# Sliding-window attention and a highway layer on one core: constants set up early, separate PSUM buffers for H and Z, x of two duos transposed by DMA

## The chip, the core and the metric

The kernel runs on one core of a Trainium2 chip. A core has five engines that run their own instruction streams and wait for each other by semaphores: TensorE (PE, matmuls, with weight loads as PEld), VectorE (DVE), ScalarE (ACT), GpSimd (POOL) and SyncE (SP, which here only issues DMAs). Matmul results go to PSUM, everything else lies in SBUF. The metric is the device time of one execution in microseconds, as a median of several runs. The span of a profile is a little shorter than that time (188.6 us against 190.34 us for the profiled run).

## What is computed

Eight heads of attention over 576 positions, causal, with a window of 128 and a bias that falls with the distance, and behind it a highway layer on the joined heads:

```python
# q, k, v: (8, 8, 576, 64)
scores = scale * np.matmul(q, k.transpose(0, 1, 3, 2))
rel = pos[:, None] - pos[None, :]
bias = slopes[:, None, None] * (-np.abs(rel))[None]
mask = (rel >= 0) & (rel < 128)
scores = np.where(mask, scores + bias[None], -1e9)
attn = softmax(scores)
x = (attn @ v) as (4608, 512)           # tokens x joined heads

H = np.maximum(x @ w_h, 0.0)
T = 1.0 / (1.0 + np.exp(-(x @ w_t + b_t)))
out = T * H + (1.0 - T) * x             # = T * (H - x) + x
```

## The kernel before

Two batch rows make a *duo*; there are four duos, 0 to 3. Each duo is worked on in *stages*: A (query blocks 0 and 1) and B (query blocks 2, 3 and the half block 4); duo 0 has four smaller ones, a to d. All stages together give 36 *blocks* of 128 tokens for the highway layer, 9 for each duo.

For every stage and head, TensorE computes scores (L299), ScalarE the exponential (L314), VectorE multiplies two heads with a mask (L324), TensorE multiplies with v (PV, L347), and VectorE divides by the sum (the norm, L363 and L364), which gives x of the stage. Ahead of that, q and k are transposed on TensorE (L234, L248) and copied out of PSUM (L260, L267, L273). Then each block goes through the highway layer:

```python
def f_x(m, kind, b):                    # x transposed on TensorE (L378)
    pt = ps_tile(BF16)
    for c in range(NCK):                # NCK = 4
        nc.tensor.transpose(out=pt[:, 0, c * P : (c + 1) * P],
                            in_=X[m, kind][:, b, c * P : (c + 1) * P], identity=ident[:])

def f_xe(m, kind, b):                   # and copied to SBUF by ScalarE (L386)
    xt = fx.tile([P, NCK, P], BF16, name="xt")
    nc.scalar.copy(out=xt[:], in_=TR[m, kind, b][:, 0, 0:512]...)

def f_h(m, kind, b):                    # H: first half of a PSUM tile (L394)
    az = ps_tile()
    for c in range(NCK):
        nc.tensor.matmul(out=az[:, 0, :], lhsT=XT[m, kind, b][:, c, :], rhs=wH[:, c, :], ...)

def f_u(m, kind, b):                    # u = max(H, 0) - x (L400)
    nc.vector.scalar_tensor_tensor(out=uu[:], in0=AZ[m, kind, b][:, 0, :], scalar=0.0,
                                   in1=X[m, kind][:, b, :], op0=ALU.max, op1=ALU.subtract)

def f_z(m, kind, b):                    # Z: second half of the same tile (L408, bias L410)
    az = AZ[m, kind, b]
    for c in range(NCK):
        nc.tensor.matmul(out=az[:, 1, :], lhsT=XT[m, kind, b][:, c, :], rhs=wT[:, c, :], ...)
    nc.tensor.matmul(out=az[:, 1, :], lhsT=ones1[:], rhs=bT[:], start=False, stop=True)

def f_th(m, kind, b):                   # tanh(Z / 2) (L415)
    nc.scalar.activation(out=tt[:], in_=AZ[m, kind, b][:, 1, :], func=ACTF.Tanh, scale=0.5)

def f_t(m, kind, b):                    # T = tt / 2 + 1/2 (L419)
    nc.gpsimd.tensor_scalar(out=tt[:], in0=tt[:], scalar1=0.5, scalar2=0.5, ...)

def f_g(m, kind, b):                    # the gate: u * T (L424)
    nc.vector.tensor_tensor(out=uu[:], in0=uu[:], in1=TT.pop((m, kind, b))[:], op=ALU.mult)

def f_out(m, kind, b):                  # the sum: u * T + x, in float32 (L429)
    nc.gpsimd.tensor_tensor(out=ot[:], in0=UU.pop((m, kind, b))[:], in1=X[m, kind][:, b, :], ...)

def f_st(m, kind, b):                   # four stores (L443), or two for a half block (L438)
    ...
```

PSUM is given out as four slots of two banks each, for scores, PV, transposes and the highway layer alike:

```python
psp = ctx.enter_context(tc.tile_pool(name="ps", bufs=BUFS["ps"], space=PSUM))   # 4
def ps_tile(dt=F32):
    return psp.tile([P, 2, 512 if dt == F32 else 1024], dt, name="ps")
```

All of these pieces are nodes with an engine, an estimated duration, a priority and what they depend on. A list scheduler in the kernel's Python puts them in an order when the kernel is built; the constants `SHIFT` and `LOOKS` tune its priorities. Each engine then runs its instructions in exactly that order. Loads of q, k and v convert float32 to bf16 and are issued by GpSimd (L101, L106, L113), stores by SyncE.

```python
node("ident", "POOL", 500, -120, c_ident)
node("tri", "POOL", 2200, -84, c_tri)              # triangles for the masks, set to 1 on GpSimd
...
node(("kpad", 0), "DVE", 450, 5 * T, lambda: c_kpad(0))
node(("vpad", 0), "DVE", 930, 6 * T, lambda: c_vpad(0))
...
node(("x", kb), "ACT", 590, t - 0.9 * dt, lambda kb=kb: f_xe(*kb), [("xp", kb)], take="xt", ...)
node(("h", kb), "PE", 870, t, lambda kb=kb: f_h(*kb), [("x", kb), ("wc",)], take="ps", ...)
node(("z", kb), "PE", 1100, t + 0.5 * dt, lambda kb=kb: f_z(*kb), [("h", kb), ("w", 1), ("w", 2)], ...)
```

Of the kernel before, what the change touches and what calls it, by code (L numbers as in the profile page):

```python
# [10 lines left out]
P = 128  # L11
# [3 lines left out]
def kernel(  # L15
# [36 lines left out]
    DMA_X = ()  # L52
# [4 lines left out]
        "ps": 4, "pA": 6, "pB": 3, "pf": 9, "x": 3, "xt": 5, "uu": 3, "tt": 3, "ot": 3,  # L57
# [3 lines left out]
        n: ctx.enter_context(tc.tile_pool(name="p" + n, bufs=BUFS["p" + n])) for n in "ABf"  # L61
# [59 lines left out]
    kk_f = cp.tile([P, 1], F32, name="kk_f")  # L121
    BIAS = cp.tile([P, H], F32, name="bias")
    tri = cp.tile([P, 3, P], BF16, name="tri")
    MK = cp.tile([P, H, 512], BF16, name="mk")
    cvec = cp.tile([P, H], F32, name="cvec")
# [13 lines left out]
    def c_tri():  # L139
        nc.gpsimd.memset(tri[:], 1.0)  # L140

        for cols, pat, base, cm in (
            (tri[:, 0, :], [[1, 4], [4, 32]], 0, -1),
            (tri[:, 1, :], [[-1, 4], [-4, 32]], -1, 1),
            (tri[:, 2, 0:D], [[-1, D]], -1, 1),
            (tri[:, 2, D:P], [[1, D]], 0, -1),
        ):
            nc.gpsimd.affine_select(
                out=cols, in_=cols, compare_op=ALU.is_ge, fill=0.0,
                base=base, pattern=pat, channel_multiplier=cm,  # L150
            )
# [63 lines left out]
    TR, SC, PT, AV, X, XT, AZ, UU, TT, OT = ({} for _ in range(10))  # L215
# [65 lines left out]
    def scores(m, kind, h):  # L281
# [7 lines left out]
        segs, n = STAGES[kind], 0  # L289
        while n < len(segs):  # L290
            j, qb, off = segs[n]
            two = n + 1 < len(segs) and segs[n + 1][0] == j and segs[n + 1][1] < 4
            for r in range(2):
                rows = slice(r * D, (r + 1) * D)
                if qb == 4:
                    rhs, w_ = QT[i][rows, h, 512:S], D
                else:
                    rhs, w_ = qm[rows, qb : qb + 1 + two], P * (1 + two)
                nc.tensor.matmul(  # L299
                    out=sc[:, r, o + off : o + off + w_],  # L300
                    lhsT=KT[i][rows, h, j * P : (j + 1) * P],
                    rhs=rhs, start=True, stop=True,
                )
            n += 1 + two

    def soft(m, kind, h):
        W = width(kind)
        if h % 2 == 0:
            pt = ptp[kind if W == 512 else "f"].tile([P, 2, 2, W], BF16, name="pt")
            PT[m, kind, h // 2] = pt  # L310
            for j, qb, off in STAGES[kind]:
                COL[m, h // 2, j, qb] = (pt, off)
        o = 0 if W == 512 else (h % 2) * W
        nc.scalar.activation(  # L314
            out=PT[m, kind, h // 2][:, h % 2], in_=SC[m, kind, h][:, :, o : o + W],
# [4 lines left out]
    def mask(m, kind, g):  # L320
        rep, lo, W = {"A": (4, 0, 256), "B": (2, 0, 512), "d": (2, 256, 256)}.get(kind, (2, 0, 256))
        o = PT[m, kind, g][:].rearrange("p h r (j w) -> p h (r j) w", w=W)
# [46 lines left out]
    def f_xd(m, kind, b):  # L369
        xt = fx.tile([P, NCK, P], BF16, name="xt")  # L370
        XT[m, kind, b] = xt
        nc.sync.dma_start_transpose(out=xt[:], in_=X[m, kind][:, b, :])

    def f_x(m, kind, b):
        pt = ps_tile(BF16)
        TR[m, kind, b] = pt
        for c in range(NCK):
            nc.tensor.transpose(  # L378
                out=pt[:, 0, c * P : (c + 1) * P],
                in_=X[m, kind][:, b, c * P : (c + 1) * P], identity=ident[:],  # L380
            )

    def f_xe(m, kind, b):
        xt = fx.tile([P, NCK, P], BF16, name="xt")
        XT[m, kind, b] = xt
        nc.scalar.copy(  # L386
            out=xt[:], in_=TR[m, kind, b][:, 0, 0:512].rearrange("p (c n) -> p c n", c=NCK)
        )

    def f_h(m, kind, b):  # L390
        az = ps_tile()
        AZ[m, kind, b] = az
        for c in range(NCK):
            nc.tensor.matmul(out=az[:, 0, :], lhsT=XT[m, kind, b][:, c, :], rhs=wH[:, c, :],  # L394
                             start=c == 0, stop=c == NCK - 1)

    def f_u(m, kind, b):
        uu = ft.tile([P, DM], BF16, name="uu")
        UU[m, kind, b] = uu
        nc.vector.scalar_tensor_tensor(  # L400
            out=uu[:], in0=AZ[m, kind, b][:, 0, :], scalar=0.0, in1=X[m, kind][:, b, :],
# [3 lines left out]
    def f_z(m, kind, b):  # L405
        az = AZ[m, kind, b]
        for c in range(NCK):
            nc.tensor.matmul(out=az[:, 1, :], lhsT=XT[m, kind, b][:, c, :], rhs=wT[:, c, :],  # L408
                             start=c == 0, stop=False)
        nc.tensor.matmul(out=az[:, 1, :], lhsT=ones1[:], rhs=bT[:], start=False, stop=True)  # L410

    def f_th(m, kind, b):
        tt = ft.tile([P, DM], F16, name="tt")
        TT[m, kind, b] = tt
        nc.scalar.activation(out=tt[:], in_=AZ[m, kind, b][:, 1, :], func=ACTF.Tanh, scale=0.5)  # L415

    def f_t(m, kind, b):
        tt = TT[m, kind, b]
        nc.gpsimd.tensor_scalar(out=tt[:], in0=tt[:], scalar1=0.5, scalar2=0.5,  # L419
                                op0=ALU.mult, op1=ALU.add)  # L420

    def f_g(m, kind, b):
        uu = UU[m, kind, b]
        nc.vector.tensor_tensor(out=uu[:], in0=uu[:], in1=TT.pop((m, kind, b))[:], op=ALU.mult)  # L424

    def f_out(m, kind, b):
        ot = op.tile([P, DM], F32, name="ot")
        OT[m, kind, b] = ot
        nc.gpsimd.tensor_tensor(out=ot[:], in0=UU.pop((m, kind, b))[:], in1=X[m, kind][:, b, :],  # L429
                                op=ALU.add)  # L430

    def f_st(m, kind, b):
        ot = OT.pop((m, kind, b))
        r, qb = blocks(kind)[b]
        if qb == 4:
            for r in range(2):
                row = (2 * m + r) * S + 512
                nc.sync.dma_start(out=out[row : row + D, :], in_=ot[r * D : (r + 1) * D, :])  # L438
        else:
            row = (2 * m + r) * S + qb * P  # L440
            dst = out[row : row + P, :].rearrange("(p t) n -> t p n", t=4)
            for t in range(4):
                nc.sync.dma_start(out=dst[t], in_=ot[32 * t : 32 * t + 32, :])  # L443
# [16 lines left out]
    node("tri", "POOL", 2200, -84, c_tri)  # L460
    node("cbias", "ACT", 1500, -88, c_bias, ["ident"])
    node("cvec", "DVE", 1300, -90, c_vec)
    node(("ones", 0), "DVE", 300, -85, lambda: c_ones(0))
    node("mask0", "DVE", 1900, -50, lambda: c_mask(0), ["tri", "cvec"])
    node("mask1", "DVE", 1500, 5 * T, lambda: c_mask(1), ["tri", "cvec"])
    node(("kpad", 0), "DVE", 450, 5 * T, lambda: c_kpad(0))
    node(("vpad", 0), "DVE", 930, 6 * T, lambda: c_vpad(0))
    node(("ones", 1), "DVE", 300, 7 * T, lambda: c_ones(1))
    node(("vpad", 1), "DVE", 930, 8 * T, lambda: c_vpad(1))
    node(("kpad", 1), "DVE", 450, 9 * T, lambda: c_kpad(1))  # L470
# [6 lines left out]
    HALF = {"A": (330, 1118, 1340, 420, 950), "B": (370, 1118, 1340, 960, 1080),  # L477
# [8 lines left out]
    last_pv = {}  # L486
    for m in range(ND):
# [56 lines left out]
        for kind in ORDER[m]:  # L544
# [3 lines left out]
            for g in range(H // 2):  # L548
# [12 lines left out]
                pring = "p" + (kind if W == 512 else "f")  # L561
                for hl in range(2):
                    h = 2 * g + hl
                    tk = ("s", m, kind, h if W == 512 else 2 * g)
                    if tk[3] == h:
                        hs = (h,) if W == 512 else (h, h + 1)
                        node(tk, "PE", C[0] * len(hs), tg + (hl - 1.3) * U,
                             lambda m=m, kind=kind, hs=hs: [scores(m, kind, h) for h in hs],
                             need, take="ps")
                    node(("exp", m, kind, h), "ACT", C[1], tg + (hl - 1.2) * U,  # L570
                         lambda m=m, kind=kind, h=h: soft(m, kind, h), [tk, "cbias"] + [("exp", m, kind, 2 * g)] * hl,
                         take=None if hl else pring, uses=[tk])
                node(("msk", key), "DVE", C[2], tg + U, lambda key=key: mask(*key),
# [143 lines left out]
```

The softmax here doesn't subtract the row's maximum and nothing guards it: scores larger than these inputs give would overflow.

## Time and profile before

| | value |
|---|---|
| time, median of 3 runs | 190.37 us (189.91 to 194.2) |
| span of the profile | 188.6 us |
| mean granted clock of TensorE | 0.988 |
| transposes of x on TensorE (L378) | 144, 14.2 us busy, mean 224 ns |
| their copies on ScalarE (L386) | 36, 20.5 us busy, mean 590 ns |
| the sum on GpSimd (L429) | 36, 46.7 us busy, mean 1297 ns |
| tanh waiting for u | 38.9 us in 34 waits |
| u waiting for the last matmul of Z | 26.3 us in 29 waits |

In the lines of the profile a piece is given by engine, line of the kernel, operation and tiles, as `uu<-ps,x` for u. The slices cut the span into 40 equal parts, and a digit is the busy share of a part in tenths. In the timeline the first two numbers are start and length in us, and what stands in brackets is how long the engine was idle before, and whose result ended that. Matmuls are pipelined, so a busy PE isn't always PE at its peak. In a list of busy time by stretches, the columns are the stretch, its length, the busy time of PE, PEld, DVE, ACT and POOL with the number of instructions, the granted clock, the share of the DMA engines, and GB/s.

### The profile page before, as it was taken

What the parts mean: (1) busy time and instruction counts of PE and PEld (TensorE: products, weight loads), DVE (VectorE), ACT (ScalarE), POOL (GpSimd) and SP (SyncE); (2) the same over time, 40 slices, a digit from 0 to 9 for tenths busy, and PEclk for the clock granted to TensorE, in tenths of its full rate; (3) what the DMA queues carried; (4) which work ended last, traced back from release to release, by engine and by line L of the source; (5) the groups of instructions that cost most, each with busy time, mean ns of one, the idle gap of its engine ahead of it and who ended that gap; (6) DMA issues with size and microseconds to landing.
All of it is one profiled execution on the core that took longest, in us unless ns stands there. A gap on an engine that the chain in (4) does not pass through costs nothing.

```text
span 188.6 us, 5196 instructions
## 1 busy us (share of the span) xinstructions
PE 152.3 (81%) x2108; PEld 96.1 (51%) x2132; DVE 136.9 (73%) x238; ACT 124.8 (66%) x178; POOL 122.0 (65%) x138
## 2 busy tenths in 40 slices
PE   0287769897899888899978889998988899979900
PEld 0265534554657445565654556665645565644400
DVE  5288876788859777899866678789676679764660
ACT  2557745866877777778797677886777767343310
POOL 7996424965989738977895256724264756564880
PEclk9999999999999999999999999999999999999995
DMA  4999999999999999999999912043030222433453
GB/s 164 219 183 190 162 128 133 196 190 148 185 178 225 223 197 175 139 200 225 229 172 188 103 41 76 20 99 98 20 87 26 59 70 56 103 81 86 111 128 94
DMA packets 70167, 25.50 MB, mean 135 GB/s; under 512 B 48128, under 2 KB 65024, under 8 KB 70144
## 3 DMA queue, kind: packets, MB, share of 16 engines
q0 software_dynamic: 62832, 14.68, 100.0%
q1 hardware_dynamic: 7312, 10.49, 21.1%
q8 instruction: 16, 0.26, 0.6%
q14 instruction: 7, 0.06, 0.1%
HBM read 30.41 MB, written 9.44 MB: 211 GB/s over the span
## 4 chain that ended last, share of the span: by engine, by line
PE 30%; DMA 19%; DVE 12%; ACT 12%; issue 11%; POOL 11%; SPq 1%; POOLq 1%; ACTq 0%; DVEq 0%
PE ps L394 11%; PE ps L408 10%; DMA kl<-in_k_dram 9%; DMA va<-in_v_dram 8%; DVE uu L400 7%; ACT pt L314 4%; ACT xt L386 4%; POOL ot L429 4%; DMA out_dram<-ot 3%; PE ps L410 3%; PE ps L248 2%; PE ps L347 2%; DVE pt L324 2%; ACT tt L415 2%; POOL ql L101 2%
## 5 line engine op out<-in xcount | busy, mean ns | idle before, releaser
L314 ACT ACTIVATE pt<-ps,bias 128x1024 bf16<-128x1024 f32 (+1 forms) x80 | 71.9, 951 | 6.2 <-PE ps L299 6.2
L429 POOL TENSOR_TENSOR ot<-uu,x 128x512 f32<-128x512 bf16 x36 | 46.7, 1297 | 22.9 <-DVE uu L424 22.8
L415 ACT ACTIVATE tt<-ps 128x512 f16<-128x512 f32 x36 | 21.5, 597 | 39.0 <-DVE uu L400 38.9
L400 DVE SCALAR_TENSOR_TENSOR uu<-ps,x 128x512 bf16<-128x512 f32 x36 | 24.9, 691 | 29.8 <-PE ps L410 26.3
L324 DVE TENSOR_TENSOR pt<-pt,mk 128x2048 bf16<-128x2048 bf16 (+1 forms) x40 | 43.7, 1099 | 0.7 <-ACT pt L314 0.7
L394 PE MATMUL ps<-wH,xt 128*128 128x512 bf16 x122 | 36.4, 384 | 4.2 <-ACT kt L273 0.6
L419 POOL TENSOR_SCALAR tt<-tt 128x512 f16<-128x512 f16 x36 | 26.0, 722 | 20.0 <-ACT tt L415 18.2
L408 PE MATMUL ps<-wT,xt 128*128 128x512 bf16 x143 | 36.9, 379 | 0.1
L299 PE MATMUL ps<-qt,kt 64*128 64x256 bf16 (+2 forms) x384 | 27.1, 250 | 6.4 <-ACT tt L415 3.9
L113 POOL DMA_DIRECT2D va<-in_v_dram x20 | 22.3, 1120 | 10.8 <-DMA kl<-in_k_dram 4.8
L347 PE MATMUL ps<-va,pt 128*128 128x65 bf16 (+1 forms) x576 | 24.9, 198 | 3.7 <-ACT pt L314 1.9
L364 DVE TENSOR_TENSOR x<-ps,rd 128x256 bf16<-128x256 f32 (+3 forms) x40 | 25.5, 638 | 1.4
L347 PEld LDWEIGHTS <-pt 128*128 128x128 bf16 (+1 forms) x576 | 20.5, 102 | 9.6 <-issue 5.1
L408 PEld LDWEIGHTS <-xt 128*128 128x128 bf16 x144 | 14.1, 98 | 17.2 <-issue 0.3
L424 DVE TENSOR_TENSOR uu<-uu,tt 128x512 bf16<-128x512 bf16 x36 | 21.0, 584 | 1.3 <-POOL tt L419 1.2
L394 PEld LDWEIGHTS <-xt 128*128 128x128 bf16 x144 | 12.7, 98 | 16.0 <-issue 4.6
L386 ACT COPY xt<-ps 128x512 bf16<-128x512 bf16 x36 | 20.5, 590 | 0.2 <-PE ps L378 0.2
L299 PEld LDWEIGHTS <-kt 64*128 64x128 bf16 x384 | 13.8, 96 | 12.8 <-issue 6.1
L248 PE MATMUL ps<-ident,ql 128*64 128x128 bf16 (+1 forms) x320 | 12.1, 228 | 8.0 <-DMA ql<-in_q_dram 7.5
L378 PE MATMUL ps<-ident,x 128*128 128x128 bf16 x144 | 14.2, 224 | 2.9 <-ACT tt L415 2.0
L273 ACT COPY kt<-ps 128x1024 bf16<-128x1024 bf16 x13 | 13.2, 1013 | 5.1 <-DVE qt L267 3.2
L267 DVE COPY qt<-ps 128x1024 bf16<-128x1024 bf16 x16 | 11.0, 688 | 7.6 <-PE ps L248 6.6
(42 smaller groups left out, 120.0 us busy)
## 6 DMA issues: line engine op xcount, KB each, us to landing
out_dram<-ot SPq DMA_DIRECT2D x128, 64.0 KB, 1.7
va<-in_v_dram POOLq DMA_DIRECT2D x16, 256.0 KB, 13.8
ql<-in_q_dram POOLq DMA_DIRECT2D x3, 1024.0 KB, 13.9
kl<-in_k_dram POOLq DMA_DIRECT2D x3, 1024.0 KB, 19.3
ql<-in_moe_w_h_dram SPq DMA_DIRECT2D x1, 1024.0 KB, 5.5
out_dram<-ot SPq DMA_DIRECT2D x8, 128.0 KB, 2.8
ql<-in_q_dram POOLq DMA_DIRECT2D x4, 128.0 KB, 5.8
kl<-in_k_dram POOLq DMA_DIRECT2D x4, 128.0 KB, 5.9
```

The source lines that it names most:

```text
L299: nc.tensor.matmul(out=sc[:, r, o + off : o + off + w_], lhsT=KT[i][rows, h, j * P : (j + 1) * P], rhs=rhs, start=True, stop=True,)
L314: nc.scalar.activation(out=PT[m, kind, h // 2][:, h % 2], in_=SC[m, kind, h][:, :, o : o + W], func=ACTF.Exp, bias=BIAS[:, h : h + 1], sca ...
L324: nc.vector.tensor_tensor(out=o, in0=o, in1=mk.to_broadcast([P, 2, rep, W]), op=ALU.mult,)
L347: nc.tensor.matmul(out=av[rows, hl, n * (D + 1) : (n + 1) * (D + 1)], lhsT=pt[:, hl, r, off : off + (D if narrow else P)], rhs=va[:, j, r, ...
L364: nc.vector.tensor_tensor(out=x.rearrange("p b (h d) -> p h b d", h=2), in0=av[:, :, :, 0:D], in1=rd[:, :, 0:nb].to_broadcast([P, 2, nb, D ...
L386: nc.scalar.copy(out=xt[:], in_=TR[m, kind, b][:, 0, 0:512].rearrange("p (c n) -> p c n", c=NCK))
L394: nc.tensor.matmul(out=az[:, 0, :], lhsT=XT[m, kind, b][:, c, :], rhs=wH[:, c, :], start=c == 0, stop=c == NCK - 1)
L400: nc.vector.scalar_tensor_tensor(out=uu[:], in0=AZ[m, kind, b][:, 0, :], scalar=0.0, in1=X[m, kind][:, b, :], op0=ALU.max, op1=ALU.subtract,)
L408: nc.tensor.matmul(out=az[:, 1, :], lhsT=XT[m, kind, b][:, c, :], rhs=wT[:, c, :], start=c == 0, stop=False)
L415: nc.scalar.activation(out=tt[:], in_=AZ[m, kind, b][:, 1, :], func=ACTF.Tanh, scale=0.5)
L419: nc.gpsimd.tensor_scalar(out=tt[:], in0=tt[:], scalar1=0.5, scalar2=0.5, op0=ALU.mult, op1=ALU.add)
L429: nc.gpsimd.tensor_tensor(out=ot[:], in0=UU.pop((m, kind, b))[:], in1=X[m, kind][:, b, :], op=ALU.add)
```

## The change

It has four parts, and with them a new order of everything:

- Constants early: the triangles are set to 1 by VectorE and cut in two pieces by GpSimd, and the padding of k and v is set at the start. A mask that could be added to the scores (`MKA`) is prepared too, but as `ADD_MASK` is empty no score uses it.
- In the last stage, T of all blocks but the first is computed on VectorE, and so is the last block's sum.
- H and Z get a PSUM tile each, from the same four slots, and Z no longer depends on H.
- For stages 6 to 9, which are those of duos 2 and 3, x is transposed by a DMA from SBUF to SBUF that SyncE issues, instead of by TensorE and ScalarE.

The buffers for the exponentials are laid out anew (a and b share one, c and d another). The highway layer is written for groups of up to two blocks, but every group holds one. `SHIFT` and `LOOKS` have new values, so the order on each engine differs throughout. Among other things, q and k of duo 1 are requested ahead of v of duo 0, and Z of a block comes before H. The diff, cut to its core:

```diff
-    DMA_X = ()
+    DMA_X = tuple(range(6, 10))
+    HOME = {"A": ("A", 0), "B": ("B", 0), "a": ("A", 0), "b": ("A", 256), "c": ("B", 0), "d": ("B", 256)}
+    GROUPS = {
+        "A": ((0,), (1,), (2,), (3,)), "B": ((0,), (1,), (2,), (3,), (4,)),
+        "a": ((0,), (1,)), "b": ((0,), (1,)), "c": ((0,), (1,)), "d": ((0,), (1,), (2,)),
+    }
+    ADD_MASK = ()
-        "ps": 4, "pA": 6, "pB": 3, "pf": 9, "x": 3, "xt": 5, "uu": 3, "tt": 3, "ot": 3,
+        "ps": 4, "pA": 5, "pB": 4, "x": 3, "xt": 5, "uu": 3, "tt": 3, "ot": 3,
...
-    def c_tri():
-        nc.gpsimd.memset(tri[:], 1.0)
+    def c_trim():
+        nc.vector.memset(tri[:], 1.0)
+    def c_mka():
+        nc.vector.tensor_scalar(out=MKA[:, :, 0:P], in0=bc(tri[:, 0, :], P), scalar1=BIG,
+                                scalar2=-BIG, op0=ALU.mult, op1=ALU.add)
+        for h in range(H):
+            nc.vector.tensor_scalar(out=MKA[:, h, P : 2 * P], in0=tri[:, 1, :], ...)
...
+    def f_xd(m, kind, gi):
+        bs, n, x = grp(m, kind, gi)
+        xt = fx.tile([P, 2, NCK, P], BF16, name="xt")
+        for i in range(n):
+            nc.sync.dma_start_transpose(out=xt[:, i], in_=x[:, i, :])
...
-        az = AZ[m, kind, b]
+        if i == 0:
+            AZ[m, kind, gi] = ps_tile()          # f_h has AH[m, kind, gi] = ps_tile() likewise
...
-    node("tri", "POOL", 2200, -84, c_tri)
+    node("trim", "DVE", 300, -110, c_trim)
+    node("tri", "POOL", 600, -96.5, lambda: c_tri(0), ["trim"])
+    node("tri2", "POOL", 500, -80, lambda: c_tri(1), ["trim"])
+    node("mka", "DVE", 1300, -95, c_mka, ["tri"])
-    node(("vpad", 0), "DVE", 930, 6 * T, lambda: c_vpad(0))
+    node(("vpad", 0), "DVE", 930, -70, lambda: c_vpad(0))
...
                 if stage_no in DMA_X:
-                    node(("x", kb), "SP", 700, t - 1.3 * dt, lambda kb=kb: f_xd(*kb), alln, take="xt", uses=[xo], land=500)
+                    node(("x", kb), "SP", 450 * n, t - 1.3 * dt, lambda kb=kb: f_xd(*kb), alln,
+                         take="xt", uses=[xo], land=1000 * n)
...
+                e, cost = ("DVE", (200, 340)) if last and gi else ("POOL", (750, 1350))      # T
+                end = last and gi == len(GROUPS[kind]) - 1
+                e, cost = ("DVE", (640, 1150)) if end else ("POOL", (1250, 2350))             # the sum
...
-    LOOKS = {"PE": 70, "ACT": 0, "DVE": 109, "POOL": 178, "SP": 159}
+    LOOKS = {"PE": 572, "ACT": 0, "DVE": 237, "POOL": 304, "SP": 712}
     # SHIFT: twenty new values
```

## The prediction

> **What bounds the kernel now.** I read the page first (busy shares and slices), then busy time by stretches, then the timeline of one period in the steady part, and last the timeline of the end.
>
> ```profile
> PE 152.3 (81%) x2108; PEld 96.1 (51%) x2132; DVE 136.9 (73%) x238; ACT 124.8 (66%) x178; POOL 122.0 (65%) x138
> ...
> PE   0287769897899888899978889998988899979900
> ...
> DMA  4999999999999999999999912043030222433453
> ```
>
> TensorE is the busiest engine, at eight to nine tenths from slice 10 almost to the end. Before that the loads set the pace: the DMA row stays at 9 for 23 slices, some 108 us, and is then nearly free. Busy time by stretches (PE is the second number) says the same in us:
>
> ```profile
> 30.00:35.00 5.00, 4.98 (x40) 2.47 (x39) 2.85 (x7) 2.50 (x5) 2.95 (x4) 1.00 1.91 160
> ...
> 100.00:110.00 10.00, 8.36 (x105) 5.30 (x104) 7.50 (x12) 7.32 (x11) 3.70 (x5) 1.00 1.26 120
> ...
> 140.00:150.00 10.00, 8.36 (x93) 5.17 (x92) 7.47 (x13) 8.09 (x12) 5.17 (x4) 1.00 0.21 53
> ...
> 180.00:188.60 8.60, 0.00 (x0) 0.00 (x0) 2.25 (x3) 0.60 (x1) 3.49 (x4) 0.74 0.44 108
> ```
>
> TensorE lacks 1.6 us in each ten at 100 and at 140 us, where no load holds it, and it does nothing after 180. The timeline of one period shows what it waits for at 100:
>
> ```profile
> 103.61 0.38 PE L410 MATMUL ps<-bT,ones 128*128 128x512 bf16 x1
> ...
> 103.83 0.39 PE L378 MATMUL ps<-ident,x 128*128 128x128 bf16 x4
> 104.03 0.69 DVE L400 SCALAR_TENSOR_TENSOR uu<-ps,x 128x512 bf16<-128x512 f32 x1 [1.05 <-PE ps L410]
> ...
> 104.81 0.60 ACT L415 ACTIVATE tt<-ps 128x512 f16<-128x512 f32 x1 [0.96 <-DVE uu L400]
> ...
> 105.31 0.58 ACT L386 COPY xt<-ps 128x512 bf16<-128x512 bf16 x1
> 105.46 0.40 PE L299 MATMUL ps<-qt,kt 64*128 64x256 bf16 x8 [0.45 <-ACT tt L415]
> ```
>
> H and Z share one PSUM tile. So u (L400), which needs H alone, waits for the last matmul of Z; tanh (L415), which needs Z alone, waits for u; and the next scores wait for the tile to come free. The pattern repeats every 4.05 us (scores at 101.41, 105.46 and 109.51).
>
> The end is a chain of single operations:
>
> ```profile
> 178.93 0.38 PE L410 MATMUL ps<-bT,ones 128*128 128x512 bf16 x1
> ...
> 180.14 0.60 ACT L415 ACTIVATE tt<-ps 128x512 f16<-128x512 f32 x1 [1.35 <-DVE uu L400]
> 180.82 0.62 POOL L419 TENSOR_SCALAR tt<-tt 128x512 f16<-128x512 f16 x1 [0.21 <-ACT tt L415]
> 181.40 1.15 POOL L429 TENSOR_TENSOR ot<-uu,x 128x512 f32<-128x512 bf16 x1
> 181.47 1.36 DVE L424 TENSOR_TENSOR uu<-uu,tt 128x512 bf16<-128x512 bf16 x1 [0.58 <-POOL tt L419]
> 182.91 1.15 POOL L429 TENSOR_TENSOR ot<-uu,x 128x512 f32<-128x512 bf16 x1 [0.36 <-DVE uu L424]
> 184.40 1.11 SPq L438 DMA_DIRECT2D out_dram<-ot  x2
> ```
>
> From TensorE's end (178.93 + 0.38 = 179.3) to 188.6 are 9.3 us.
>
> **What the Trainium skill says.** (1) "VectorE: DVE Perf Modes", section "The three transpose paths": a 128x128 bf16 transpose takes 390 ns on TensorE and 1309 ns through the DMA crossbar. The trace has 224 ns on average for the first, and four back to back occupy 0.33 us in the chain; it has no DMA transpose. (2) "DMA: Bandwidth & Descriptors", section "Anatomy of one DMA": a fixed cost near 2.0 us (stated for transfers issued by GpSimd). The stores here, issued by SyncE, land in a median 1.7 us, so I estimate 2 to 4 us for a transposed block from issue to landing, from these two places. (3) "GPSIMD Engine Reference", section "Key points": it shares its SBUF interfaces with VectorE and contends with two-input operations. The trace agrees: the gate at 181.47 took 1.36 us beside GpSimd's sum, other gates 0.42; the sum took 2.06 us in places against 1.15 alone.
>
> **The change part by part.**
>
> *x by DMA in duos 2 and 3.* 18 of 36 blocks leave TensorE and ScalarE: 18 x 0.33 = 5.9 us of TensorE, 18 x 0.59 (L386) = 10.6 us of ScalarE. What comes in is 18 transfers on SyncE's queue. There is room: in the SyncE waits the stores (L443) wait 114 us in total for GpSimd, and these duos' blocks come after the loads have ended at 108 us. The built order places the transposes ahead of the matmuls that use them, with five buffers. At the last stage the first two can start only when all of x is normalized; there TensorE has about 2.8 us of earlier blocks' matmuls (H, Z, H) to cover 3.5 to 4 us.
>
> *Separate tiles.* u can follow H, and tanh can follow Z, without each other. Each is a whole slot of the four, so a block takes three slots (two with DMA) where it took two, but holds H's for about 0.86 + 0.69 and Z's for 1.08 + 0.60 instead of one for the sum. In the built order Z comes before H, so the last operation after TensorE is u, not tanh. The waits of TensorE for tanh between 50 and 166 us (L299 3.7, L378 1.2, L394 0.5) sum to 5.4 us. I credit 3, as the slots stay four.
>
> How far the two may go together: within the 4.05 us period TensorE does transposes 0.32, scores 2 x 0.32, PV 0.40, H 0.86, Z 1.08: 3.30. Without transposes it is 2.98. VectorE in the same period has a mask 1.22, a norm 0.20 + 0.69, u 0.69, the gate 0.42: 3.22, and with waits between them some 3.5. So in the late duos VectorE takes over before all of TensorE's saving arrives. I let 80% of 5.9 through: 4.7.
>
> *The end.* From the last H: u 0.69, gate 0.42, sum on VectorE at most 0.69 (like u), 0.2 between them, and then what stands from the sum's end (184.06) to 188.6 today, 4.5: together 6.5 against 9.3, so 2.8 less. GpSimd also loses four scalings of 0.62 in the last stage.
>
> *The start.* Memsets go to VectorE's idle beginning. The mask that would be added (mka) is built but nobody reads it: nine operations, about 1.4 us by the durations of the mask copies (0.59 for 128x1024), while VectorE waits for loads anyway. More matters what the new order does to the loads: q and k of duo 1 are now asked for before v of duo 0. The first v landed at 26.2 us; now 2.1 MB more lie ahead of it, and at the 190 GB/s of the early slices that is 11 us, so I estimate 37. TensorE does not lose that time: by then it can do the transposes of duo 0 (8 x 1.06) and of duo 1 (8 x 0.61) and the scores of three stages (about 4), some 18 us, and by my count from the durations once it is warm the kernel before has done about 18 us of work at 35. So the start costs about 2 us.
>
> **Sum.** 190.4 - 4.7 (transposes) - 3.0 (separate tiles) - 2.8 (end) + 2.0 (start) = 181.9. As a cross-check from TensorE's side: the work after 37 us is about 149 - 18 = 131 us (155 before, by these durations, less 6). At 95% density it ends at 37 + 138 = 175, plus 6.5 of end, plus 1.8 that the time has over the span: 183. I say **182 us**.
>
> **Rivals.**
>
> 1. *VectorE becomes the bound at once, or the four slots stall.* For it: 3.22 us of 4.05, and up to six slot requests for each period of duo 1 where there were five. Against it: VectorE sat idle 26.3 us waiting for L410, and that wait goes. Then the steady part gains 2 us instead of 7.7, and the time is about 187 to 188.
> 2. *DMA transposes are late.* For it: a transfer takes longer than 1 us of TensorE and ScalarE together, and SyncE's queue runs in order, so a transpose stands behind a store that waits for GpSimd's sum. Against it: the queue is mostly idle, and the transposes are planned ahead. If each of the four stages lost 2 us at its first block: 190.
> 3. *v is late.* If the small rows of v, which ran at 128 to 133 GB/s, land only at 41 us, TensorE idles four more us: 186.
> 4. *It goes better.* If TensorE becomes dense (97%) after 37 us: 37 + 135 + 6.5 + 1.8 = 180; with v at 35, 178.
>
> **Range and chances.** Single rivals 1 and 3 lie at 186 to 188, rival 2 at 190, the good case at 178. Each rival seems to me less likely than one in five, so the range is 177 to 188. The 2% line is at 186.6: faster 0.80, same 0.15, slower 0.05.
>
> **What would show each step.** Right: in the list of waits, none of u for the bias matmul and none of tanh for u; TensorE at 146 us busy and ScalarE at 114; transposes of x absent after 120 us with TensorE's wait for DMA below 3 us in all; 6 to 7 us from TensorE's last matmul to the end; first PV near 37 us. Wrong: TensorE waiting for xt by DMA several us in each late stage, or first PV after 41 us, or tenths of TensorE that stay at 8 between 50 and 165 us with VectorE now at 9.

## The result, and the profile after

The changed kernel takes 192.95 us (median; 192.81 to 196.26), 1.0146 times the kernel before (95% interval 1.0113 to 1.0178). It is slower by 1.5%, where 4% faster was predicted. Some executions of either kernel fall into a slower state, as that of 196.26 us, and are left out of the ratios and of the medians in the table below. The span is 191.3 us against 188.6.

The page of the changed kernel, busy shares and slices:

```profile
PE 152.3 (80%) x2060; PEld 88.8 (46%) x2060; DVE 140.5 (73%) x253; ACT 117.3 (61%) x160; POOL 125.1 (65%) x132
...
PE   0286869789999429999999999999999999299500
...
PEclk9999999999999965999999999999999999969985
```

A slice is 4.8 us. TensorE is now at 9 almost everywhere from slice 10 on, but with two holes that were not there before: "42" at 62 to 72 us, and "2" at 163 to 167. After each hole the granted clock drops and matmuls take longer. That is part of why TensorE's busy time has not fallen although it has fewer matmuls; in addition, the profile before lacks some records (122 of the 144 matmuls of H are there). The end ("500") is longer too. The same in busy time by stretches of the changed kernel (PE is the second number, the granted clock the seventh):

```profile
60.00:70.00 10.00, 4.48 (x68) 2.70 (x66) 8.42 (x11) 5.23 (x7) 6.24 (x5) 0.94 1.54 213
70.00:80.00 10.00, 9.44 (x106) 5.41 (x107) 2.96 (x5) 5.33 (x7) 6.70 (x6) 0.72 2.15 187
140.00:150.00 10.00, 9.87 (x121) 5.24 (x121) 9.23 (x15) 7.31 (x10) 7.88 (x7) 1.00 0.53 123
165.00:170.00 5.00, 2.72 (x8) 1.07 (x9) 2.40 (x4) 0.60 (x1) 3.09 (x4) 0.78 0.61 138
```

At 140 us TensorE is busy 9.87 of 10 us, where it was 8.36: the steady part did become dense. The 5 us lost at 60 to 70 and the 2.3 us at 165 to 170 are what is new. Its waits name the releasers (total us, times, longest):

```profile
ACT tt L468 <- PE ps L462: 35.9, 26, 5.4
...
POOL ot L484 <- DMA out_dram<-ot: 11.1, 7, 2.2
...
PE ps L270 <- DMA kl<-in_k_dram: 8.1, 3, 5.5
...
PE ps L460 <- DMA xt<-x: 4.8, 3, 3.4
```

ScalarE's tanh now waits for its own matmul (the bias, L462), not for u: the 38.9 us of waits for u are gone. In their place come one wait of 5.5 us for k, waits of TensorE for an x transposed by DMA, and 11.1 us in which GpSimd's sum waits for stores to free its output buffer.

One mark divides the runs well: the start of the last PV on TensorE, behind which only the highway layer of the last blocks is left. It comes at 164.28 us before and at 158.15 after. So the change gains 6.1 us up to there, and loses 8.8 us behind it (24.3 us from the mark to the end before, 33.1 after).

### The profile page after: what moved, and what is told of

Same layout as the page of the kernel before. It is cut to its first block, busy times and chain, and to the rows that moved or that the text cites. A ratio compares the mean times of both kernels' runs of the same rounds, so it can differ in the third digit from the quotient of the medians.

```text
span 191.3 us, 5107 instructions
## 1 busy us (share of the span) xinstructions
PE 152.3 (80%) x2060; PEld 88.8 (46%) x2060; DVE 140.5 (73%) x253; ACT 117.3 (61%) x160; POOL 125.1 (65%) x132
## 4 chain that ended last, share of the span: by engine, by line
PE 43%; DMA 28%; DVE 7%; ACT 7%; SPq 5%; POOL 4%; issue 2%; POOLq 0%; DVEq 0%; ACTq 0%
DMA kl<-in_k_dram 24%; PE ps L460 12%; PE ps L443 10%; PE ps L386 6%; PE ps L328 5%; PE ps L270 5%; SPq L500 4%; ACT pt L344 4%; ACT kt L295 3%; PE ps L462 3%; DMA xt<-x 3%; DVE pt L363 3%; POOL ql L110 2%; DVE qt L289 2%; DMA out_dram<-ot 2%
## 5 line engine op out<-in xcount | busy, mean ns | idle before, releaser
L484 POOL TENSOR_TENSOR ot<-uu,x 128x512 f32<-128x512 bf16 x35 | 53.2, 1520 | 30.0 <-DVE uu L478 18.2
L363 DVE TENSOR_TENSOR pt<-pt,mk 128x2048 bf16<-128x2048 bf16 (+1 forms) x40 | 46.0, 1162 | 0.3 <-ACT pt L344 0.3
L460 PE MATMUL ps<-wT,xt 128*128 128x512 bf16 x144 | 38.7, 392 | 5.9 <-DMA xt<-x 4.8
L443 PE MATMUL ps<-wH,xt 128*128 128x512 bf16 x144 | 38.5, 391 | 0.2
L473 POOL TENSOR_SCALAR tt<-tt 128x512 f16<-128x512 f16 x32 | 23.2, 726 | 8.7 <-ACT tt L468 8.5
L478 DVE TENSOR_TENSOR uu<-uu,tt 128x512 bf16<-128x512 bf16 x36 | 17.5, 485 | 6.7 <-POOL tt L473 4.9
L460 PEld LDWEIGHTS <-xt 128*128 128x128 bf16 x144 | 12.4, 99 | 20.7 <-DMA xt<-x 6.3
L270 PE MATMUL ps<-ident,kl 128*64 128x128 bf16 (+1 forms) x320 | 13.0, 241 | 8.8 <-DMA kl<-in_k_dram 8.1
L270 PE MATMUL ps<-ident,ql 128*64 128x128 bf16 (+1 forms) x320 | 13.0, 238 | 8.7 <-DMA ql<-in_q_dram 8.2
L289 DVE COPY qt<-ps 128x1024 bf16<-128x1024 bf16 x16 | 11.1, 691 | 11.7 <-PE ps L270 10.3
L443 PEld LDWEIGHTS <-xt 128*128 128x128 bf16 x144 | 12.3, 100 | 13.8 <-issue 3.1
L270 PEld LDWEIGHTS <-ql 128*64 128x64 bf16 (+1 forms) x320 | 10.6, 132 | 11.2 <-DMA ql<-in_q_dram 8.5
```

The lines of the kernel that those rows point to most:

```text
L270: nc.tensor.transpose(out=pt[r * D : (r + 1) * D, c : c + n], in_=L[ps, r, nh * hs + hl, t * D : (t + 1) * D], identity=ident[ps, ps],)
L363: nc.vector.tensor_tensor(out=o, in0=o, in1=mk.to_broadcast([P, 2, rep, W]), op=ALU.mult,)
L443: nc.tensor.matmul(out=AH[m, kind, gi][:, i, :], lhsT=XT[m, kind, gi][:, i, c, :], rhs=wH[:, c, :], start=c == 0, stop=c == NCK - 1)
L460: nc.tensor.matmul(out=az, lhsT=XT[m, kind, gi][:, i, c, :], rhs=wT[:, c, :], start=c == 0, stop=False)
L473: eng.tensor_scalar(out=tt, in0=tt, scalar1=0.5, scalar2=0.5, op0=ALU.mult, op1=ALU.add)
L484: eng.tensor_tensor(out=ot[:, 0:n, :], in0=UU.pop((m, kind, gi))[:, 0:n, :], in1=x, op=ALU.add)
```

## The experiments

| run | what it is | last PV, us | span, us | time, us (median) | time / time before [95%] |
|---|---|---|---|---|---|
| before | | 164.28 | 188.6 | 190.14 | 1 |
| after | | 158.15 | 191.3 | 192.87 | 1.0146 [1.0113, 1.0178] |
| e1_hoist | after, last transposes issued ahead of stores | 158.34 | 192.4 | 194.26 | 1.016 [1.0047, 1.0272] |
| e2_last_pe | after, last stage's x on TensorE | 157.31 | 185.5 | 187.47 | 0.984 [0.9725, 0.9955] |
| e3_act_st | after, half of duo 3's stores issued by ScalarE | 158.43 | 185.8 | 187.62 | 0.9825 [0.9704, 0.9946] |
| e4_no_k2 | after, k of duo 2 not loaded | 152.39 | 186.0 | 187.74 | 0.9855 [0.9739, 0.997] |
| e5_shared | after, H and Z in one tile again | 163.23 | 195.8 | 196.09 | 1.0276 [1.019, 1.0363] |
| e7_all_pe | after, all x on TensorE | 163.30 | 188.4 | 188.91 | 0.9873 [0.9787, 0.9959] |
| e8_late_tr | after, transposes of duo 2's first q, k later | 158.28 | 191.5 | 193.53 | 1.015 [1.0066, 1.0234] |
| e9_late_tr2 | the same, at a better place | 154.78 | 187.9 | 189.63 | 0.9919 [0.9889, 0.9949] |
| c1_three | e2, e3 and e9 together | 154.08 | 181.8 | 182.27 | 0.9573 [0.949, 0.9656] |
| b1_sep | before, with separate tiles alone | 158.09 | 180.8 | 182.88 | 0.9579 [0.9508, 0.965] |
| f1_sep_end | b1, and the end on VectorE | 158.33 | 180.6 | 181.88 | 0.9533 [0.9463, 0.9604] |
| f2_sep_end_dma | f1, and 13 transposes by DMA | 154.26 | 176.6 | 177.73 | 0.932 [0.9245, 0.9395] |

The span and the mark are those of one execution. Executions of one kernel lie up to 2.7 us apart (e1_hoist: 192.26 to 195.0 us), so a difference of 1 or 2 us between two spans shows little by itself. The mark is steadier: where nothing ahead of it should differ, it lies at 158.15, 158.34 and 158.43 us (after, e1, e3), and at 158.09 and 158.33 (b1, f1).

### The end: a late place in the queue, or too little time on SyncE

The timeline of SyncE in the changed kernel (start, time for which it issues with the short pauses between the issues of one row, what, how many):

```profile
164.78 2.54 SPq L418 DMA_TRANSPOSE xt<-x  x2
167.41 1.93 SPq L500 DMA_DIRECT2D out_dram<-ot  x4
169.45 1.20 SPq L418 DMA_TRANSPOSE xt<-x  x1
170.74 1.93 SPq L500 DMA_DIRECT2D out_dram<-ot  x4
172.77 1.19 SPq L418 DMA_TRANSPOSE xt<-x  x1
174.06 1.92 SPq L500 DMA_DIRECT2D out_dram<-ot  x4
176.08 1.19 SPq L418 DMA_TRANSPOSE xt<-x  x1
177.37 9.70 SPq L500 DMA_DIRECT2D out_dram<-ot  x20
187.18 1.14 SPq L492 DMA_DIRECT2D out_dram<-ot  x2
```

And what TensorE did when the first of these transposes had landed, with its idle time before in brackets:

```profile
167.28 1.38 PE L460 MATMUL ps<-wT,xt 128*128 128x512 bf16 x4 [3.37 <-DMA xt<-x]
```

The last norm of the stage had ended at 160.93 us; its first transpose went out at 164.78, behind stores. On SyncE there is next to no gap. A block needs one transpose (1.19 to 1.27 us of SyncE) and four stores (1.93 us), 3.2 us together (its turn comes every 3.3 us: 169.45, 172.77, 176.08), while TensorE needs 1.95 us for H and Z of a block there. From 151.22 to 188.32 us the rows of SyncE sum to 35.8 of 37.1 us. That suggests the theory called S, that SyncE has too little time. Its rival, Q, is that the transposes merely stand behind stores that wait for GpSimd. Changing only the order tells them apart.

**e1_hoist.** On SyncE, the first four transposes of the last stage are issued right behind the stage's last norm, ahead of the waiting stores.

```diff
+    at = ("nrm", (3, "B", 3))
+    for gi in range(4):
+        put(("x", (3, "B", gi)), at)      # put: move in the order, behind the second
+        at = ("x", (3, "B", gi))
```

> The changed kernel, with one difference: on SyncE, the first four transposes of x of the last stage come before the stores of the stage ahead of it instead of between them. Theory S (SyncE is short of time at the end: a block's four stores take it 1.93 us and a transpose 1.2 to 1.3 us, and from 151 us on it is busy without a gap): the same issues are still in the queue, so the time changes by less than 2 us (191 to 194), although TensorE finishes some 4 us sooner. Rival Q (SyncE has time enough, but transposes stand behind stores that wait for a sum on GpSimd): about 6 us less, 186 to 188.

The timeline of SyncE in this run:

```profile
164.90 5.13 SPq L418 DMA_TRANSPOSE xt<-x  x4
170.12 1.18 SPq L492 DMA_DIRECT2D out_dram<-ot  x2
171.39 5.70 SPq L500 DMA_DIRECT2D out_dram<-ot  x12
177.20 1.22 SPq L418 DMA_TRANSPOSE xt<-x  x1
```

TensorE and GpSimd, a little later:

```profile
173.38 1.15 POOL L484 TENSOR_TENSOR ot<-uu,x 128x512 f32<-128x512 bf16 x1 [5.91 <-DMA out_dram<-ot]
176.62 1.86 PE L460 MATMUL ps<-wT,xt 128*128 128x512 bf16 x4 [3.22 <-DVE uu L450]
```

The four transposes now follow each other in one piece of 5.13 us. The first two come no earlier than before (from 164.90 us, against 164.78), as the eight stores ahead of them stayed there. The third and fourth come 2.0 and 4.0 us earlier, and the stores later instead. GpSimd's sum then waits 5.91 us for stores to free its buffer, and through the scaling, the gate and u TensorE stops for 3.22 us. The span is 192.4 us: no gain, as S said, though S also expected TensorE to finish some 4 us sooner, and it finished 1.3 us later (181.94 against 180.65). So Q falls for the transposes that could be moved; for the first two this run does not decide it.

**e2_last_pe and e3_act_st** take the load off SyncE in two ways: five transposes fewer, or half of the stores issued by another engine.

```diff
 # e2: the node "x" of stage (3, "B")
-    f_xd(*kb)
+    f_x(*kb); f_xe(*kb)                  # TensorE and ScalarE, at the same place
 # e3: block stores of duo 3 (the half block's stores: all on nc.scalar)
-    nc.sync.dma_start(out=dst[t], ...)
+    (nc.scalar if m == 3 and t % 2 else nc.sync).dma_start(out=dst[t], ...)
```

> The changed kernel, with x of the last stage alone transposed on TensorE and copied by ScalarE as before; the order of all else is kept. Theory S: 5 x 1.25 = 6.3 us leave SyncE's queue in the stretch where it is dense, and TensorE takes on 5 x 0.33 = 1.7 us, so 5 to 6 us less: 187 to 188. Rival Q: the same direction, about 6 us less, as no transpose stands behind a store of this stage. If the end has nothing to do with SyncE: no change or 1 us more.

> The changed kernel, with two of the four stores of each block of duo 3 (and both of the half block) issued by ScalarE, which has little to do at the end. All transposes stay on SyncE. Theory S: some 8 us of issue time leave SyncE after 162 us, its queue is no longer dense, and TensorE's last matmul comes 5 us sooner: 184 to 187. Rival Q: the transposes still stand behind stores that wait for the same sums, so little changes: 191 to 193.

Both took 5.5 to 5.8 us off the span, and 5.3 to 5.4 off the median time. So it is SyncE's load, whichever way it is relieved: e3 leaves every transpose on SyncE and moves as many bytes. (e3 gives half of the stores another queue as well as another issuing engine. That the issuing and not the queue's transfers set the pace is read from the rows above, where SyncE issues without a gap; the run does not separate the two.) In e3 TensorE still stops for 3.10 us for its first x, and finishes only 1.8 us sooner, not the 5 that were expected: most of the gain is that the stores behind it are out sooner. The Trainium skill, "DMA: Bandwidth & Descriptors", section "Issuing engines are not separate DMA queues", says that issuing from several engines saves only the sequencer's time, "which is usually small relative to the DMA itself". Here the trace differs: that time filled 35.8 of the last 37.1 us, and moving half of the stores to another engine was worth 5.5 us. Whether fewer and larger stores, or more output buffers, would help as much was not tried.

Some of it remains in e2, which keeps the transposes of the stage before. GpSimd's timeline in e2, 5.5 us behind the mark:

```profile
162.83 1.15 POOL L484 TENSOR_TENSOR ot<-uu,x 128x512 f32<-128x512 bf16 x1 [3.38 <-DMA out_dram<-ot]
```

The sum waits for stores that stand behind those transposes (one of these stores also held SyncE for 1.7 us, which the profile does not explain), and through the scaling, the gate and u TensorE waits 3.42 us there.

**e7_all_pe** puts all x back on TensorE (as e2, for stages 6 to 9).

> The changed kernel, with x of all blocks transposed on TensorE and copied by ScalarE, in the places of the order that the DMA transposes had. Theory S: all 18 transposes, 22 us of SyncE, are gone, and TensorE has 5.9 us more to do, of which some 4 lie before the last PV, where it is dense. So the end is shorter than with the last stage alone on TensorE, the middle longer by 4 us: 186 to 190 in all, below the changed kernel. If the DMA transposes were a gain where SyncE has time: 2 us or more above the run with the last stage alone on TensorE (188.2).

It measures what the DMA transposes do as a whole. With them (after) the mark comes 5.15 us earlier (158.15 against 163.30). Only 13 of the 18 lie ahead of it, which is 13 x 0.33 = 4.3 us of TensorE; in e7 k of duo 2 also came 0.6 us later (see below). Behind the mark they cost 8.0 us (33.1 against 25.1). Together they make the changed kernel 2.9 us longer by the spans, 4.0 by the median times. And e2 against e7, with the 13 alone: 6.0 us at the mark, but 2.9 at the span and 1.4 in the median time. In this order even those pass on half of what they gain, or less.

### The hole at 65 us: k of duo 2

TensorE in the changed kernel:

```profile
64.39 0.64 PE L270 MATMUL ps<-ident,ql 128*64 128x128 bf16 x16 [0.55 <-DMA ql<-in_q_dram]
70.56 1.06 PE L270 MATMUL ps<-ident,kl 128*64 128x128 bf16 x16 [5.53 <-DMA kl<-in_k_dram]
71.55 1.89 PE L460 MATMUL ps<-wT,xt 128*128 128x512 bf16 x4
```

It stood still for 5.53 us until k of duo 2 had landed, and then ran slowly: four matmuls of Z in 1.89 us, elsewhere 1.03. The Trainium skill, "TensorE: Matmul & The Clock Gate", section "HAM oscillation — how this bites in real kernels", says that TensorE's clock is halved after an idle gap of more than about 3.4 us; the trace agrees, with a granted clock of 0.50 from 70 to 74 us. k of duo 2 lands at 70.5 us, hardly earlier than before (issued at 51.62 us, landed after 19.3 us, at 70.9). What is new is that TensorE asks for it at 65 us, and as it runs in order, everything behind waits. In the kernel before, the first transposes of this k were:

```profile
77.08 0.61 PE L248 MATMUL ps<-ident,kl 128*64 128x128 bf16 x16
```

By then Z of nine blocks was done; in the changed kernel, at 65 us, of six. So it is the new order that asks too early, not a faster TensorE: b1_sep (below), with the old order and a denser TensorE, asks at 76.8 us and has no such stop.

**e4_no_k2** leaves out the load of k of duo 2 (1 MB), so that its output for that duo is computed from what lay in the buffer.

```diff
+        if m == 2 and w == 1:
+            return
```

> The changed kernel without the load of k of duo 2: its scores use the k of duo 0 that lies in the buffer, so the output of duo 2 is not the reference's. 1 MB of 14.7 in the loads is left out, and TensorE has nothing to wait for at 64 us. Theory K (the stop of 5.5 us at 65 to 70.5 us and the half clock that follows it to 75 us cost the span some 8 us): 6 to 8 us less, 185 to 187, with the mean granted clock at 0.97 to 0.98. Rival: the next loads (v of duo 2, q and k of duo 3) stop TensorE instead, or SyncE's queue at the end takes the gain: less than 3 us.

5.8 us came off at the mark and 5.3 off the span (5.1 off the median time), less than the 6 to 8 expected. At the end TensorE then stopped for 4.58 us for its first x by DMA, where it was 3.37. The run also takes 1 MB of traffic away, so the 5.8 us at the mark are an upper value for the stop.

**e8_late_tr and e9_late_tr2** keep the load and move only the first transposes of duo 2's q and k, and their copies, to a later place in the order.

```diff
 # e8
+    at = ("g", (0, "d", 0))               # behind this block's gate
 # e9
+    at = ("th", (0, "d", 1))              # behind this block's tanh
+    for key in (("tr", 2, 0, (None, 0)), ("te", 2, 0, (None, 0)),
+                ("tr", 2, 1, (None, 0)), ("te", 2, 1, (None, 0))):
+        put(key, at)
+        at = key
```

> The changed kernel, with the first transposes of q and k of duo 2 and their copies set later in the order, behind some 4 us of TensorE's work of duos 0 and 1 that stood behind them. Theory K2 (the stop at 65 us is one of order: k lands at 70.5 us as in the kernel before, and TensorE runs in order): the stop falls from 5.5 us to 1 to 2 us, the half clock goes or is shorter, and the time falls by 3 to 5 us, to 188 to 190. Rival L (the loads set the pace up to 100 us): TensorE only waits later, for the next k or v, and the time changes by less than 1.5 us.

> As the run before it with q and k of duo 2 transposed later, but now the copy of q on VectorE stands ahead of the gate that waited for GpSimd there. (In that run TensorE worked on to 70.4 us, but then stood 4.5 us, as the copy of q stood behind a gate, and the gate behind GpSimd, which waited to issue a load of v.) Theory K2 (the stop is one of order): the stop is below 1.5 us, the last PV comes 3 to 5 us sooner than 158.2, and the time is 188 to 190, as without the load of k. Rival L (the loads set the pace): another stop takes its place again, and the time stays within 1.5 us of 193.

e8 was a miss. TensorE in e8:

```profile
70.74 0.64 PE L270 MATMUL ps<-ident,ql 128*64 128x128 bf16 x16 [0.65 <-DVE uu L450]
75.91 1.06 PE L270 MATMUL ps<-ident,kl 128*64 128x128 bf16 x16 [4.53 <-DVE qt L289]
```

k had landed, but the copy of q (L289) now stood on VectorE behind a gate that waited for GpSimd, so a stop of 4.53 us took the place of the old one. With the copy ahead of that gate (e9) the stop shrank to 0.80 us (another, of 1.54 us, followed at 75 to 77 us), and the span to 187.9, 3.4 less. The order in which TensorE, VectorE and GpSimd meet at this place thus decides 3.4 us.

**c1_three** joins e2, e3 and e9.

> The changed kernel with three repairs together: x of the last stage on TensorE, half of duo 3's stores issued by ScalarE, and q and k of duo 2 transposed later (as in the run beside it). Theory S with K2: the two losses are independent, so the gains add: 193 - 5 (either repair of SyncE) - 1 to 2 (the other one) - 4 (order) = 182 to 183. If they are one loss told twice: 187 to 188.

181.8 us, 9.5 less than the changed kernel (10.6 by the medians). Two separate losses fit this, one loss told twice does not: e2 or e3 (5.5 to 5.8) and e9 (3.4) add up to 8.9 to 9.2.

### Separate tiles, alone and in the changed order

**e5_shared** puts H and Z of the changed kernel back into one tile, in the changed order; **b1_sep** gives Z its own tile in the kernel before, and changes nothing else.

```diff
 # e5: f_h and f_z
-    AH[m, kind, gi] = ps_tile();  AZ[m, kind, gi] = ps_tile()
+    if (m, kind, gi) not in AZ:
+        AZ[m, kind, gi] = ps_tile()       # H in [:, 0, :], Z in [:, 1, :]
 # b1: f_z of the kernel before
-    az = AZ[m, kind, b]
+    az = ps_tile()
+    AZ[m, kind, b] = az                   # H's tile is kept as AH, f_u reads that
```

> The changed kernel, with H and Z of a block in the two halves of one PSUM tile again; the order is the changed one. Theory T (the tiles of their own are what made TensorE dense between 80 and 158 us, 98% against 91% before): TensorE falls back to 90 to 93% there and the time rises by 3 to 6 us, to 196 to 199. Rival P (the four slots are the limit, and a shared tile takes one where two were taken): no more than 1 us of change.

> The kernel before with one part of the change alone: H and Z get a PSUM tile each, from the same four slots; its order is kept. Theory T: u no longer waits for Z nor tanh for u, and 3 to 5 us of TensorE's waits go: 186 to 188. Rival P: three slots for a block where two were taken make TensorE wait for slots as long as it did for the shared tile, or longer: 190 to 195.

Both runs show the same thing: by the mark the separate tiles are worth 5.1 us in the changed order (163.23 against 158.15) and 6.2 in the old one. In the changed order 4.5 us of this reach the span, and 3.2 the median time. Alone they make the span 180.8 us, 7.8 less than before, ratio 0.958, more than theory T expected (3 to 5). The timeline of one period of b1 shows how:

```profile
105.46 0.68 DVE L400 SCALAR_TENSOR_TENSOR uu<-ps,x 128x512 bf16<-128x512 f32 x1
...
105.55 0.38 PE L413 MATMUL ps<-bT,ones 128*128 128x512 bf16 x1
...
106.03 0.60 ACT L418 ACTIVATE tt<-ps 128x512 f16<-128x512 f32 x1 [0.42 <-PE ps L413]
...
106.09 0.40 PE L299 MATMUL ps<-qt,kt 64*128 64x256 bf16 x8
```

u (L400) starts before the bias matmul of Z (L413) and tanh starts before u has ended (106.03 against 106.14). The next scores start at 106.09, 0.54 us after the bias matmul; before, it took 1.85 us (103.61 to 105.46). From one H to the next here it is 3.40 us (103.82 to 107.22), against a period of 4.05.

### The end on VectorE, and DMA transposes where SyncE has time

**f1_sep_end** adds to b1 the change's end: T of the last stage's blocks but the first, and the last block's sum, on VectorE.

```diff
-    nc.gpsimd.tensor_scalar(out=tt[:], ...)     # T, blocks 1 to 4 of stage (3, "B")
+    nc.vector.tensor_scalar(out=tt[:], ...)
-    nc.gpsimd.tensor_tensor(out=ot[:], ...)     # sum, block 4
+    nc.vector.tensor_tensor(out=ot[:], ...)
```

> The kernel before with two parts of the change: tiles of their own for H and Z (182.9 alone), and in the last stage T of all blocks but the first and the last block's sum on VectorE. From the prediction's working for the end: 2 to 2.8 us less than with the tiles alone, 180 to 181. Rival: the stores, 1.93 us of SyncE's time for each block against 1.95 of TensorE, already pace the end, and the gain is below 1 us.

180.6 against 180.8 us of span, and 1.0 us by the median times: at most about 1 us, where 2 to 2.8 were expected. The last store issue starts at 176.38 us in f1 and at 176.62 in b1. Even with plain stores SyncE issues without a gap there (16 in 8.13 us in f1), so a sum that is ready earlier has to wait its turn. The kernel before shows the same at its end:

```profile
176.52 7.78 SPq L443 DMA_DIRECT2D out_dram<-ot  x16
```

These issues end at 184.30 us, and the last two follow at 184.40.

**f2_sep_end_dma** adds DMA transposes to f1 for stages 6, 7 and 8 (13 blocks) but not for the last stage. Each is issued a block ahead, at the place of the previous block's transpose on TensorE.

```diff
+    for st in ((2, "A"), (2, "B"), (3, "A")):
+        # ("xd", block 0): right behind the stage's last norm
+        # ("xd", block b): where block b - 1 was transposed on TensorE
+        # ("xp", b), ("x", b) of TensorE and ScalarE: dropped
```

> The run beside it (tiles of their own, end on VectorE), and x of stages 6 to 8 transposed by DMA, each block's transfer issued one block ahead; the last stage stays on TensorE. Theory S: SyncE has time here (13 transposes by 1.25 us between 110 and 160 us), so the 13 x 0.33 = 4.3 us that leave TensorE arrive for the most part: 3 to 4 us less than the run beside it, 176 to 178. Rival: the transfer's 2.5 us are not covered at the head of each of three stages, and 2 us or less arrive.

4.0 us less of span than f1 (4.1 by the medians), where 13 x 0.33 = 4.3 us of TensorE were taken away. The timeline of SyncE in f2 shows the room, and where it ends:

```profile
147.80 1.93 SPq L446 DMA_DIRECT2D out_dram<-ot  x4
149.84 2.50 SPq L372 DMA_TRANSPOSE xt<-x  x2
152.43 2.42 SPq L446 DMA_DIRECT2D out_dram<-ot  x4
154.95 2.40 SPq L441 DMA_DIRECT2D out_dram<-ot  x2
157.45 15.11 SPq L446 DMA_DIRECT2D out_dram<-ot  x32
```

The last transposes are out by 152.3 us, and the stores that follow have SyncE to themselves. TensorE's weight loads wait 0.4 us in all for an x by DMA. f2 is the best version: 177.73 us (median), 0.932 times the kernel before (0.9245 to 0.9395), and 0.92 times the changed one by the medians.

## Why the prediction was wrong, point by point

**The step that failed: "There is room."** The prediction read the 114 us for which SyncE's stores wait for GpSimd as free time of the queue. It is a sum over the kernel, with a single wait of 41.6 us in it. The transposes of the last stage fall into a stretch where each block brings 3.2 us of issuing, against 1.95 us of TensorE. The prediction had estimated how late a transpose lands (2 to 4 us; measured, a median of 2.5 us) and never how long it holds SyncE. As e2 and e3 show, that one omission is worth 5.5 to 5.8 us of span. For the first transposes of the last stage it expected 2.8 us of matmuls to cover 3.5 to 4 us from issue to landing. Landing took 2.5, but the issue came 3.85 us after the last norm, and TensorE stood for 3.37. Its own rival 2 had the right place ("a transpose stands behind a store that waits for GpSimd's sum") but the wrong mechanism (SyncE was busy, not waiting), and put 2 us on each of four stages; the loss that e2 removed lay in the last one alone.

**The transposes, -4.7.** Right up to the mark: 5.15 us (e7 against after), though it counted all 18 blocks and only 13 lie ahead of the mark. Wrong for the whole: +2.9 us, because of the 8.0 us behind it. With the last stage left on TensorE and in the old order, the gain arrives (f2: 4.0 of 4.3 us).

**Separate tiles, -3.0.** Right in its mechanism: tanh no longer waits for u. In the changed order they brought 5.1 us at the mark, and 4.5 of span or 3.2 of time (e5), not far from the number; alone they brought 7.8 of span (b1). The prediction credited only those waits of TensorE that name tanh, 5.4 us, and took off some for the four slots. It left out that every block's chain became shorter. TensorE's busy time from 80 to 155 us rose from 68.22 to 73.71 of 75 us with this alone. That VectorE would then take over did not happen: at 140 us it is busy 9.23 of 10 us in the changed kernel, and TensorE still 9.87.

**The end, -2.8.** Wrong: the end grew. The changed kernel's last operations on VectorE and SyncE:

```profile
180.76 0.69 DVE L450 SCALAR_TENSOR_TENSOR uu<-ps,x 128x512 bf16<-128x512 f32 x1 [1.57 <-PE ps L443]
...
182.14 0.42 DVE L478 TENSOR_TENSOR uu<-uu,tt 128x512 bf16<-128x512 bf16 x1
...
184.44 0.69 DVE L484 TENSOR_TENSOR ot<-uu,x 128x512 f32<-128x512 bf16 x1 [1.88 <-DMA out_dram<-ot]
187.18 1.14 SPq L492 DMA_DIRECT2D out_dram<-ot  x2
```

The operations are as short as predicted (0.69, 0.42, 0.69), but between gate and sum stand 1.88 us of waiting for a store to free the buffer, and between sum and store 2.05 us in SyncE's queue. From TensorE's end (179.62 + 1.03) to 191.3 it is 10.6 us, predicted 6.5, before 9.3. With the transposes gone, the same step still brings only 0.2 us of span, or 1.0 of time (f1 against b1): the stores pace the end. In the kernel before they already did, as its last 16 stores show, and the prediction, which counted the time from the last sum to the end as fixed, did not see it.

**The start, +2.0.** The first PV in the changed kernel, and a wait in the kernel before:

```profile
35.30 0.42 PE L386 MATMUL ps<-va,pt 128*128 128x65 bf16 x8
26.23 0.54 PE L347 MATMUL ps<-va,pt 128*128 128x65 bf16 x7 [1.50 <-DMA va<-in_v_dram]
```

The prediction took the second line for the landing of the first v. It is that of the second part; the first PV before came at 22.84 us. So the delay was 12.5 us, estimated 11, and that 35.3 came near the predicted 37 is partly luck. As said, TensorE did not lose that time: up to 60 us it was busy for 43.45 us, and for 43.75 in the kernel before. But the account stopped there. The same reasoning, "what is asked for, and when does it land", was needed once more at duo 2, whose k lands as late as ever and is asked for earlier in the new order. That is the 3.4 us (e9) to 5.3 us (e4) that no term and no rival held.

**The two losses together.** With both taken away (c1) the median time is 182.27 us, where 182 was predicted. (c1 also has x of the last stage back on TensorE.) So SyncE's time and the stop for k make up nearly all of the miss; that the rest agrees to 1 us is luck, as the terms were off in both directions.

**What the terms leave.** e7 and f1 have the same parts (separate tiles, the end on VectorE, no DMA transposes) and differ in the new order, the buffers and the early constants: 188.4 against 180.6 us of span, 7.0 us by the median times. The stop for k may account for 3.4 to 5.3 of these 7.0 to 7.8 us. The other 1.7 to 4.4 us were not taken apart; the early constants and the new order weren't tried one by one. The unused mask cost VectorE 1.6 us, from 14.7 us on, while it had nothing else to do.

## What to carry to other kernels

Count what a queue's issuing costs for each piece of work in the stretch where it is needed, and set it against the pace of the engine that it has to keep up with; a sum of waits over the kernel is not room, and landing time is not issue time. Two results that different engines read are better kept in different PSUM tiles, if there are slots for them; here that alone, in the old order, was worth more than all the rest of the change. When the order of an engine changes, look for every load that it will now ask for earlier, and for when that load lands.

## What the runs showed of the hardware that was not expected

- In the changed kernel a DMA transpose of 128x512 bf16 (128 KB) from SBUF to SBUF held SyncE for 1.19 to 1.30 us; a store of 128 KB (those of the half blocks) held it for about 0.57 us (1.14 / 2 at 187.18 us), one of 64 KB for about 0.48 us (1.93 / 4). From issue to landing they took a median of 2.5, 2.4 and 1.8 us. So transpose and store of the same size differ in issuing and hardly in landing.
- TensorE ran at half clock not only after a stop of 5.53 us but also after shorter ones. After that of 3.37 us in the last stage of the changed kernel four matmuls of H took 1.91 us instead of 1.03, with a granted clock of 0.50 from 168 to 170 us. In c1_three a stop of 2.96 us was followed by four matmuls of Z in 1.91 us, with a clock of 0.50 from 164 to 166 us.
